# A hand-ordered two-layer kernel on one core: the skip term D of the first unit as rank-one matmuls, all spectral steps of two units summed, and a new instruction list

## The chip, the cores and the metric

The kernel runs on one core of a Trainium2 chip. Five engines work side by side, each through its own queue and strictly in the order in which its instructions were written: TensorE (PE in the profile; its weight loads are shown apart as PEld), VectorE (DVE), ScalarE (ACT), GpSimd (POOL) and SyncE (SP), which here does nothing but begin transfers. The metric is the device time of one execution in microseconds (us).

## The reference, cut to what matters

The input has 2048 positions of 640 channels, in bf16. Layer A normalises `q`, scales and shifts it by a modulation, and multiplies it by a long convolution; layer B is a gated MLP with a matmul over positions.

```python
k_shift = sum of 4 shifted copies of k, each times shift_k
kv = k_shift * v
y  = irfft(rfft(kv, 2S) * rfft(ssm_k, 2S))[:S]      # long convolution over positions, per channel
y  = y + kv * ssm_D                                 # skip term D, one number per channel
x  = x + ga * (LN(x)*(1+ca)+sa) * y                 # layer A
h  = LN(x)*(1+cb)+sb                                # layer B
z  = gelu(h @ w_in);  z1, z2 = halves;  z2 = LN(z2)
x  = x + gb * ((z1 * (w_sp @ z2 + b_sp)) @ w_out)
```

## The kernel before, in words

**Work and stages.** The 640 channels are cut into five *units* of 128 (`NU`, `DU`). For each unit, two sequences go through a Fourier transform made of matmuls: the filter (`XK`, from `ssm_k`) and the product `kv` (`XU`). A first stage (`stage1`, op `s1`) gives the tile `X1`; then come eight *steps* per sequence, each covering two blocks of frequencies:

- `fwd` on PE (`forward`): six matmuls into the PSUM tile `pu`. For the filter, ACT then copies the spectrum into the tile `KH` (`khc`).
- `prod` on DVE (line 454): the four real products of the spectrum of `kv` in PSUM with `KH`, 1024 elements in each partition.
- In a *summed* step (mode `s`) the products go to an f32 tile `Tf`, and two additions (`csum`, line 468, on POOL or DVE) turn them into the real and the imaginary part, tile `W`; the inverse (`inv`) is then six matmuls. In an *unsummed* step (mode `u`) the products go to a bf16 tile `T`, and `inv` does the additions itself, with twelve matmuls.
- `zc` copies the result of the inverse from PSUM to the tile `Z` on ACT or DVE.

After the eight steps `Z` is transposed (by a transfer `zt` for units 0 to 3, by PE in `last_stage_pe` for unit 4), and `y` (op `y` or `yl`) gives the convolution, which DVE multiplies into `gh` (`ym`, `yml`, lines 670 and 732). `gh` holds the modulated first normalisation (`xn`, `ghm`, line 653). The sum into `xt` is `res` (line 690), its statistics are `ln2`, `ag2`.

`kv` itself comes from transposing transfers of `k` and `v` (`load_kv`, op `ldk`), four tap matmuls (`taps`) with diagonal weights (`diag`), the product with `v` on DVE (`tv`, line 545), a write to DRAM (`kvw`) and a read in another layout (`load_X`, op `ldX`). The matrices of the transform are made on the chip: `F1` by DVE and ACT (`f1a`, `f1c`, `f1m`), `M2` by DVE, ACT and POOL (`turns`, `msub`, `msin`, `msgn`, `mneg`), `G2` by transposing `M2` (`gflip`, `gcopy`, `gneg`).

**The skip term** is put into the filter: `add_D` (op `addD`, line 392) adds D to position 0 of each channel's filter, after a chain in which D is loaded (`Dr`), spread (`dwide`), turned by PE (`turn1 tD`) and copied (`dcol`). Stage 1 of the filter waits for it.

**Layer B's first half** takes over after unit 4: normalisation (`zx`), a turn by PE (`hfl`) or by a transfer, modulation (`hmod`), the product with `w_in` (`zz`, 64 of five matmuls of 432 columns each, into `pu` or `pz`), `gelu` on ACT, normalisation `zn`. The second half (lines 961 to 1039) multiplies by `w_sp` (line 968) and `w_out` (line 989).

**What sets the order.** All of this up to the end of layer B's first half is registered as some thousand numbered operations with their dependences (class `Plan`). The string `ORDER` lists them, each with the engine that does it (P, A, D, G, S for PE, ACT, DVE, POOL, SP), and the kernel writes the instructions in just this order. So the list fixes each engine's queue and also which engine does an operation that several could do (the registered letters, `"GD"` for `csum`, say which may). PSUM tiles rotate: `pu`, `pz` and `sm` have two buffers each, `s1` one, so a matmul waits until the engine that reads the older tile is done. `FILLS` are matmuls without use, put into PE's queue at chosen places.

The choice of mode, and the inverse of a summed step:

```python
mode = MODE[u][st]; summed = mode == "s"
...
mm(p_[:, k], G2[:, 0, kc, :], w_[:, k], True, False)        # summed: 3 matmuls for each of 2 blocks
mm(p_[:, k, 1], G2[:, 2, kc, :], w_[:, k, 0], False, False)
mm(p_[:, k, 0], G2[:, 1, kc, :], w_[:, k, 1], False, True)
```

Of the kernel before, what the change touches and what calls it, by code (L numbers as in the profile page):

```python
# [11 lines left out]
BF16 = mybir.dt.bfloat16  # L12
# [3 lines left out]
P = 128  # L16
# [9 lines left out]
DU = 128  # L26
KP = 2
# [6 lines left out]
FILLS = (4, 3, 3, 2, 4, 3, )  # L34
MODE = ('susussus', 'susussus', 'susussus', 'susussus', 'susussus')
# [5 lines left out]
D0 G5 D13 S82 A1 S2 D15 D100 A4 D14 P1029 P7 G101 A16 D102 D109 D110 D6 D103 S19 D17 P1030 P8 D11 A111 A112 D121 D86  # L41
P1031 P145 A146 P148 A150 A149 D10 D23 D122 A123 D18 S88 G113 D90 S21 A124 G125 D147 D104 A106 G114 D115 S83 D87 A105
G126 P1032 P227 S20 A228 S22 P26 D27 P24 P154 A155 D116 A118 A117 S523 P151 A153 S34 D25 S32 P30 D31 P233 A234 P28 D29
S33 D152 A156 S35 G107 P133 D134 S84 S85 G119 G120 P139 P229 A140 S524 P161 D527 P163 A162 D528 G108 P136 D137 A164
P165 A166 P142 G48 A143 S46 S47 P157 A158 P169 A170 A230 G36 P37 P167 A168 G135 D529 P41 D530 P159 A160 D127 D38 G138
D144 P171 A172 P231 D42 D232 P173 P176 A175 A174 A177 P43 A178 D44 P182 A183 A184 P179 D181 P39 D40 S45 A180 P185 A531
D186 S3 P195 A532 A533 G187 P55 D196 P191 D192 D56 P211 P51 P247 A248 G197 G188 G198 P189 A190 P199 A200 P9 A12 D212
G213 D52 P205 D206 P201 P53 D202 G214 A534 D54 P49 D50 P217 S526 A542 A543 P245 A246 S89 D535 P193 A194 A544 G130 G131
S565 P251 G141 D218 D252 G72 P203 P221 D222 P239 A240 G207 G536 D537 P215 A204 G223 G224 A216 P253 D254 P568 P566 S525
P241 A242 P257 P225 A258 G553 G554 A569 P237 P249 G549 G550 A238 A250 S91 P255 A256 D538 D539 P219 S57 D226 D93 G208  # L50
D540 D541 P235 A236 P243 A244 P301 A302 A551 G60 G555 P259 P209 D260 G261 G262 A567 P291 D292 S570 G552 P303 S58 P269
A304 A220 D270 G271 S92 D210 P571 G272 D572 P285 D286 P307 A308 A545 P263 S59 P265 D266 P573 P63 P275 D276 A264 P305
A306 P293 A294 D546 P273 A274 D574 D649 P325 D64 G556 G287 D288 D709 D591 D651 G593 G547 D548 D557 D558 G559 G560 A326
P309 A310 P267 A268 P321 A322 P327 P315 A316 P65 D66 P319 A328 A561 G562 P61 D62 A320 A128 P295 S575 S70 D296 G297 S71
P329 A330 P576 P578 S94 D129 G298 D577 D592 D594 P313 A314 G653 P331 A332 D579 S599 P67 D68 P311 A312 A563 S69 S95
P289 A290 P333 D96 G564 D595 G596 P349 D711 P375 A376 P299 A300 D334 G335 G336 D350 P73 D74 S97 P379 A380 P77 P323
A324 P343 D344 P377 A378 P369 P337 A338 P351 A352 P317 A318 G597 G598 D78 G345 G346 P600 P381 D370 G371 P279 P347 G652
D601 P602 D280 G281 G282 A382 P277 D612 A348 P365 D603 D366 P79 D80 G655 P387 A278 P604 G372 A388 P399 A400 P359 P283
A284 P383 A384 D614 D605 P606 D360 D613 P401 P373 A402 G618 D619 P385 A386 D650 P353 P403 D354 A404 P339 G361 G362
D340 P75 D76 A374 P397 A398 P405 A406 G615 P367 D607 P395 A396 P407 D99 G616 D617 P449 S580 A450 A368 P413 G608 D408  # L60
P341 A342 P389 A390 P363 A364 D414 S620 P621 D672 P453 A454 G609 P393 A394 D622 P623 D624 P439 D440 G355 G356 S81 S98
P451 G409 P391 P625 P357 P427 A452 D626 P627 A392 D358 S657 G654 G410 P455 A456 P417 D428 P581 A582 D418 P411 A412
G676 G677 P457 A458 P473 A474 P471 A472 G429 D430 P443 P431 A432 P479 A480 P433 D628 P415 A416 G419 D444 S583 G629
D631 P475 A476 G420 P421 D434 P461 A462 P423 D670 D656 P477 A478 D424 P467 A468 G713 P658 D659 A422 P441 P463 A464
G445 D446 G671 P660 D661 G435 G436 A442 P481 D482 G634 D637 G674 P437 A438 P465 A466 P447 A448 P662 P497 P425 A426
P517 D663 P664 D498 G483 G484 P485 G675 D518 G519 A486 S754 P507 D508 D665 D633 P469 A470 P499 D509 A500 P459 A460
G520 G510 P501 D502 P521 G666 P487 D488 A522 S678 P511 A512 P513 D514 P584 A585 P491 G673 P489 A490 P515 G503 G504
A516 G712 P505 D492 G493 D494 D638 P679 D680 D635 G707 A506 P495 P681 D682 A496 P721 D630 G708 P683 D684 P719 D720
P685 A722 D686 G687 P717 P715 D716 A718 D632 S586 P587 A588 D688 D689 P723 D724 G710 D725 D727 D726 D756 D755 G757
D728 D729 D636 D730 D758 A759 P589 A590 P732 D733 G760 D690 D768 P746 G692 P1033 P1034 P761 D691 P762 D763 G667 D764  # L70
D765 A767 D731 D769 G770 P739 D734 D736 D738 A766 D695 D735 P813 A814 D771 G772 A773 D737 D833 D693 D696 D694 D832
S753 P781 P815 A816 P809 D831 A782 D834 G714 D747 P774 D777 D776 P775 A780 P788 G835 D836 G837 D840 A810 A789 A779
G838 D778 D740 D741 D744 D743 P791 A792 A839 S841 D697 G668 D701 D698 D700 P811 A812 P819 A820 P817 P795 D699 D745
# [970 lines left out]
```

## Time and profile before

| what | us |
|---|---|
| median of 3 runs (320.10 to 321.21) | 320.46 |
| the profiled execution, its own time | 320.46 |
| its span, from the first to the last instruction | 318.6 |
| around the span | 1.86 |
| PE busy | 307.7 |
| DVE busy | 209.3 |
| ACT busy | 146.2 |
| POOL busy | 124.1 |
| first product of unit 0 (`prod`) begins | 28.80 |
| last product of unit 4 ends | 119.16 |
| first matmul of layer B (`zz`) begins | 131.55 |
| first matmul of line 968 begins | 190.67 |

A line of a group gives the source line, the engine, the operation, the tiles (written <- read), the shapes (written <- read), the count after an x, the busy time, the mean duration in ns, and the idle time of that engine just before such instructions with what ended it. A line of the timeline begins with the start and the duration, both in us. A line of a table of windows gives the window, its length, the busy time of PE, PEld, DVE, ACT and POOL with the number of instructions, the granted clock, the share of the DMA engines and GB/s. The duration of a matmul includes its way through the array; so the time that a matmul costs PE is read from the distance between starts. On DVE and ACT, too, an instruction starts some 0.08 to 0.12 us before the one ahead of it has ended, when nothing is waited for.

### The profile page before, as it was taken

What the parts mean: (1) busy time and instruction counts of PE and PEld (TensorE: products, weight loads), DVE (VectorE), ACT (ScalarE), POOL (GpSimd) and SP (SyncE); (2) the same over time, 40 slices, a digit from 0 to 9 for tenths busy, and PEclk for the clock granted to TensorE, in tenths of its full rate; (3) what the DMA queues carried; (4) which work ended last, traced back from release to release, by engine and by line L of the source; (5) the groups of instructions that cost most, each with busy time, mean ns of one, the idle gap of its engine ahead of it and who ended that gap; (6) DMA issues with size and microseconds to landing.
All of it is one profiled execution on the core that took longest, in us unless ns stands there. A gap on an engine that the chain in (4) does not pass through costs nothing.

```text
span 318.6 us, 6407 instructions
## 1 busy us (share of the span) xinstructions
PE 307.7 (97%) x2575; PEld 203.5 (64%) x2575; DVE 209.3 (66%) x436; ACT 146.2 (46%) x259; POOL 124.1 (39%) x157
## 2 busy tenths in 40 slices
PE   7898999999999998999999999999999999999995
PEld 2475787878899987655555555555555555555554
DVE  8897999898999999997669682522222333323323
ACT  4889898987798755777657671000000000000001
POOL 2651879779988996884163310000000000000000
PEclk9999999999999999999999999999999999999999
DMA  8999999997967685030409980676557555522221
GB/s 162 223 224 256 273 289 191 224 250 175 229 173 141 238 161 217 2 71 14 83 0 159 192 202 19 132 156 117 116 115 117 115 117 115 115 51 49 49 51 62
DMA packets 127024, 44.99 MB, mean 141 GB/s; under 512 B 116143, under 2 KB 126228, under 8 KB 126996
## 3 DMA queue, kind: packets, MB, share of 16 engines
q1 hardware_dynamic: 126842, 44.55, 65.0%
q8 instruction: 20, 0.33, 0.4%
q14 instruction: 8, 0.07, 0.1%
q10 hardware_dynamic: 154, 0.05, 0.1%
HBM read 16.11 MB, written 5.24 MB: 67 GB/s over the span
## 4 chain that ended last, share of the span: by engine, by line
PE 75%; DVE 11%; SPq 6%; DMA 4%; POOL 2%; ACT 1%; issue 1%; DVEq 0%; POOLq 0%
PE ps L968 29%; PE pu L237 14%; PE pz L237 13%; PE po L989 9%; SPq L513 5%; PE sm L237 4%; DVE Tf L454 3%; PE s L237 3%; DMA big<-in_A_k_dram 2%; DVE T L454 2%; DMA X<-in_A_ssm_k_dram 1%; DVE big L545 1%; DVE X L240 1%; POOL W L468 1%; DVE T L337 1%
## 5 line engine op out<-in xcount | busy, mean ns | idle before, releaser
L968 PE MATMUL ps<-X,wT 128*128 128x432 bf16 x512 | 95.7, 346 | 0.0
L968 PEld LDWEIGHTS <-wT 128*128 128x128 bf16 x512 | 50.1, 98 | 42.2
L981 ACT COPY uT<-pt 128x896 bf16<-128x896 bf16 x1 | 0.9, 906 | 119.2 <-PE pt L980 119.2
L237 PEld LDWEIGHTS <-Z 128*128 128x128 bf16 x320 | 31.1, 98 | 26.8 <-DVE Z L857 0.2
L237 PE MATMUL pu<-X,M 128*128 128x128 bf16 (+1 forms) x480 | 45.9, 237 | 1.0 <-DVE Tf L454 0.5
L237 PEld LDWEIGHTS <-M 128*128 128x128 bf16 x480 | 37.6, 98 | 7.9 <-issue 2.2
L971 DVE SCALAR_TENSOR_TENSOR u<-ps,bcol,G 128x432 bf16<-128x432 f32 x18 | 12.0, 668 | 42.2 <-PE ps L968 42.2
L468 POOL TENSOR_TENSOR W<-Tf 128x256 bf16<-128x256 f32 x45 | 33.1, 752 | 16.0 <-DVE Tf L454 14.1
L237 PE MATMUL pu<-big,Z 128*128 128x432 bf16 x160 | 33.3, 346 | 0.0
L989 PE MATMUL po<-w_o,uT 128*128 128x320 bf16 (+2 forms) x231 | 33.2, 295 | 0.1
L237 PE MATMUL pz<-big,Z 128*128 128x432 bf16 x160 | 33.1, 346 | 0.0
L454 DVE TENSOR_TENSOR Tf<-pu,KH 128x1024 f32<-128x1024 f32 x25 | 30.3, 1219 | 2.1 <-PE pu L237 1.6
L240 ACT CAST X<-s 128x1024 bf16<-128x1024 f32 x29 | 29.7, 1024 | 3.7 <-PE s L237 3.4
L989 PEld LDWEIGHTS <-uT 128*128 128x128 bf16 (+1 forms) x231 | 22.2, 98 | 9.9 <-issue 0.2
L971 DVE SCALAR_TENSOR_TENSOR u<-ps,bcol,M 128x432 bf16<-128x432 f32 x14 | 9.3, 667 | 28.9 <-PE ps L968 28.9
L240 ACT CAST KH<-pu 128x512 bf16<-128x512 f32 x40 | 23.4, 598 | 6.2 <-PE pu L237 4.9
L237 PEld LDWEIGHTS <-G 128*128 128x128 bf16 x330 | 24.7, 98 | 1.8 <-issue 0.2
L991 DVE TENSOR_TENSOR ot<-po,xt 128x320 bf16<-128x320 f32 (+1 forms) x33 | 15.9, 481 | 12.6 <-PE po L989 12.6
L240 ACT CAST Z<-pz 128x512 bf16<-128x512 f32 x37 | 21.5, 596 | 5.6 <-PE pz L237 5.6
L237 PEld LDWEIGHTS <-X 128*128 128x128 bf16 x288 | 17.7, 97 | 6.7 <-DVE X L392 3.6
L237 PE MATMUL sm<-big,dg 128*128 128x512 bf16 (+1 forms) x80 | 20.2, 379 | 0.8 <-DMA big<-in_A_k_dram 0.8
L912 DVE BATCH_NORM_STATS2 stz<-X 128x6 f32<-128x432 bf16 x32 | 17.6, 585 | 4.4 <-ACT X L906 4.4
(150 smaller groups left out, 432.7 us busy)
## 6 DMA issues: line engine op xcount, KB each, us to landing
wm<-in_w_mod_dram SPq DMA_DIRECT2D x6, 800.0 KB, 6.9
xt<-in_A_q_dram SPq DMA_DIRECT2D x4, 640.0 KB, 5.8
out_dram<-ot SPq DMA_DIRECT2D x15, 160.0 KB, 2.3
big<-in_B_w_in_dram SPq DMA_DIRECT2D x2, 1080.0 KB, 7.8
X<-in_A_ssm_k_dram SPq DMA_DIRECT2D x4, 512.0 KB, 5.5
kv_scr<-big SPq DMA_DIRECT2D x4, 512.0 KB, 5.6
X<-kv_scr SPq DMA_DIRECT2D x4, 512.0 KB, 5.0
w_o<-in_B_w_out_dram SPq DMA_DIRECT2D x6, 160.0 KB, 3.2
```

Of the source, the lines that this page charges most:

```text
L237: nc.tensor.matmul(o, lhsT=w, rhs=x, start=start, stop=stop)
L240: (e.copy if e is nc.scalar else e.tensor_copy)(dst, src)
L337: op("D", "msub", lambda e: e.scalar_tensor_tensor(tl[a][:], tl[a][:], MAGIC, tl["mbase"][:, None].to_broadcast([P, 2, KCH, QH]), op0=ALU. ...
L454: e.tensor_tensor(T_[:], (tl[pu] if src is None else tl[src])[:, :, :, None, :].to_broadcast(shape), tl[KH][:, :, None, :, :].to_broadcast ...
L468: e.tensor_tensor(tl[W][:, :, o, :], T_[:, :, 0, o, :], T_[:, :, 1, 1 - o, :], op=ALU.add if o else ALU.subtract)
L513: e.dma_start_transpose(tl[name][:, o + h * m:o + (h + 1) * m], src[0, h * m:(h + 1) * m, dt * P:(dt + 1) * P])
L545: e.tensor_tensor(vsl, tl[ps][:], vsl, op=ALU.mult)
L912: op("D", "stz", lambda e, i=i, n=n, fc=fc: e.bn_stats(out=stz[:, n, fc, :], in_=tl[z2][:, i, fc * FC:(fc + 1) * FC]), r=[(z2, (i, fc))], ...
L968: nc.tensor.matmul(ps[:, :FC], lhsT=wTs[t][:, s_, :], rhs=tl["z2_%d" % (s_ // TB)][:, s_ % TB, fc * FC:(fc + 1) * FC], start=(s_ == 0), st ...
L971: nc.vector.scalar_tensor_tensor(u[:, sl], ps[:, :FC], bcol[:, t:t + 1], z1[t][:, sl], op0=ALU.add, op1=ALU.mult)
L989: nc.tensor.matmul(ps[:, :hi - lo], lhsT=uTs[t][:fsz[ft], ft, :], rhs=w_o[:fsz[ft], ft, lo:hi], start=(ft == 0), stop=(ft == NFT - 1))
L991: nc.vector.tensor_tensor(ot[:, lo:hi], ps[:, :hi - lo], xt[:, t, lo:hi], op=ALU.add)
```

## The change

1. **D of unit 0.** `add_D` is no longer called for unit 0. A tile `oneD` of one partition holds 128 ones (written by POOL) and D of the unit's 128 channels (one more small transfer, `ld1`, begun by SP). Each of unit 0's eight `fwd` of the filter gets one more matmul for each of its two blocks, with one row of weights, the ones, and the 128 values of D as the moving operand: it adds D to the real part of every frequency.
2. **Modes.** In units 0 and 1 all eight steps are summed, in place of five of eight; the other units stay as they are.
3. **First normalisation.** Tiles 2 and 3 (of each 8) may now be done by ACT as well.
4. **Fills.** Eight groups of 21 matmuls in place of six groups of 19: six groups with 16 before unit 0's spectrum is begun (before: four with 12), and two with 5 ahead of the first `yl` (before: two with 7 behind the third `yl`).
5. **A new list.** It assigns and orders everything anew. By engine it differs mainly in this: DVE gets 11 `csum` in place of 5, 19 `ghm` for 17, 4 `zc` for 3, 10 `zx` for 5, two `s1` copies more, 9 `zn` for 12 and one `xn`, one `gcopy`, the one `gneg`, the one `diag` and two `addD` fewer. POOL gets 51 `csum` for 45, 21 `ghm` for 23, 10 `xn` for 11, 2 `zx` for 7. ACT gets one `diag`, one `gcopy`, two `xn`, three `zn` more. On SP the order changes in few places: the new transfer of `oneD` stands after the second half of unit 0's filter, ahead of the second halves of `k` and `v` of unit 0; the small transfer of `c` moves from behind unit 1's `kvw` to ahead of unit 1's `v`; the load of `w_mod`'s first part moves ahead of `XU1`; the two halves of `w_in` change places.

```diff
-FILLS = (4, 3, 3, 2, 4, 3, )
-MODE = ('susussus', 'susussus', 'susussus', 'susussus', 'susussus')
+FILLS = (4, 3, 1, 2, 4, 2, 4, 1, )
+MODE = ('ssssssss', 'ssssssss', 'susussus', 'susussus', 'susussus')
...
+        oneD = consta.tile([1, 2, DU], BF16, name="oneD")
...
         def forward(name, X1, st, extra=()):
+            with_D = X1 == "X1K0"
+
...
-                    mm(pu[:, k, 1], M2[:, 1, kc, :], x[:, 2 * kc, :], False, True)
+                    mm(pu[:, k, 1], M2[:, 1, kc, :], x[:, 2 * kc, :], False, not with_D)
+                    if with_D:
+                        mm(pu[:, k, 0], oneD[:, 0], oneD[:, 1], False, True)
...
-            op("D" if n % 8 < 4 else "DA" if n % 8 == 4 else "A", "ln1", stats, r=xs, w=[("mv1", n), ("gh", (0, n // TB))], new=[(tile_, "st1")])
+            op("D" if n % 8 < 2 else "DA" if n % 8 < 6 else "A", "ln1", stats, r=xs, w=[("mv1", n), ("gh", (0, n // TB))], new=[(tile_, "st1")])
...
+        op("G", "dzero", lambda e: e.memset(oneD[:, 0], 1.0), w=[("oneD", 0)])
+        op("S", "ld1", lambda e: e.dma_start(oneD[:, 1], A_ssm_D[None, 0:DU]), w=[("oneD", 1)])
...
-            add_D(u)
+            if u:
+                add_D(u)
```

The queues of the new list where the prediction steps through them (numbers behind a name are unit and step; `s1 K0.0` is stage 1 of unit 0's filter, first quarter):

- PE, start: fill 4, `tsk`, fill 3, `s1 K0.0`, `s1 K0.4`, `taps 0.1`, fill 1, `tD`, fill 2, `s1 K1.0`, fill 4, fill 2, `s1 K0.12`, `s1 K0.8`, `s1 K1.4`, `taps 0.3`, `0.2`, `0.0`, then seven `fwd` of K0 among the four `gflip`, `s1 K1.12`, `tc`, `taps 1.3`, `s1 U0.0`, `U0.4`, `taps 1.0`, `s1 U0.8`, `U0.12`, `taps 1.2`, `fwd U0.0`.
- DVE, start: `ident`, `bits0`, `f1a`, `f1g`, `mstep`, `mbase`, `f1m`, `turns 1`, `turns 3`, `msub 3`, `dwide`, `msub 1`, `bits2`, `e2a`, `dcol`, `addD K1`, `turns 0`, `tv 0.1`, `msub 0`, `turns 2`, `msub 2`, `tv 0.3`, `mneg`, `tv 0.2`, `tv 0.0`.
- ACT, start: `silut`, `f1c`, `skc`, `diag 0`, all eight `s1` copies of K0 among the eight `msin`, one `s1` copy of K1, then the seven `khc` among three `gcopy`.
- End of unit 4: the last product is that of step 6 (unsummed; before, step 2, summed), then `inv 4.6`, `y`, `inv 4.2`, and the four turns `zfl` in the order 16, 24, 0, 8, of whose copies ACT does three and DVE one (before two each).

## The prediction, made before the changed kernel was run

> **What bounds the kernel now.** I read the page's first two parts first.
>
> ```profile
> span 318.6 us, 6407 instructions
> ...
> PE 307.7 (97%) x2575; PEld 203.5 (64%) x2575; DVE 209.3 (66%) x436; ACT 146.2 (46%) x259; POOL 124.1 (39%) x157
> ...
> PE   7898999999999998999999999999999999999995
> ...
> DVE  8897999898999999997669682522222333323323
> ```
>
> PE is busy nearly throughout, and behind 131.55 us (slice 17 on) its matmuls follow each other without a gap: the 64 `zz` and what follows cost what they cost, and neither their number nor their shape changes. So the change can act only by moving the moment at which `zz` begins. Before that moment DVE's row is as full as PE's. The table of windows, asked from the first product of unit 0 to the end of the last one of unit 4, says how full:
>
> ```profile
> 28.80:119.16 90.36, 88.13 (x1082) 74.99 (x1079) 85.11 (x123) 74.94 (x131) 77.22 (x88) 1.00 0.97 215
> ```
>
> Of 90.36 us DVE is busy for 85.11 and idle for 5.25. PE's 88.13 counts the way through the array. By distances between starts, its matmuls of this stretch leave some 6 us of gaps. POOL is idle for 13.1. So two engines with 94% each set the pace, and no wait among them is long: in the list of waits, PE's and DVE's longest here are 0.8 us.
>
> **The change part by part.** The prices:
>
> ```profile
> L468 POOL TENSOR_TENSOR W<-Tf 128x256 bf16<-128x256 f32 x45 | 33.1, 752 | 16.0 <-DVE Tf L454 14.1 <-DVE nmr L592 1.5 <-PE sm L237 0.3
> L454 DVE TENSOR_TENSOR Tf<-pu,KH 128x1024 f32<-128x1024 f32 x25 | 30.3, 1219 | 2.1 <-PE pu L237 1.6 <-ACT gh L568 0.2 <-issue 0.2
> ...
> L454 DVE TENSOR_TENSOR T<-pu,KH 128x1024 bf16<-128x1024 f32 x15 | 18.2, 1216 | 0.6 <-PE pu L237 0.4
> ...
> L653 DVE TENSOR_TENSOR gh<-gh,gca_bf 128x512 bf16<-128x512 bf16 x10 | 4.6, 488 | 0.1
> ...
> L468 DVE TENSOR_TENSOR W<-Tf 128x256 bf16<-128x256 f32 x5 | 2.2, 444 | 0.0
> ```
>
> These are groups by shape. The next lines are from the timeline at the end of unit 4:
>
> ```profile
> 117.39 1.93 PE L237 MATMUL pz<-T,G 128*128 128x256 bf16 x24
> ...
> 117.94 1.22 DVE L454 TENSOR_TENSOR Tf<-pu,KH 128x1024 f32<-128x1024 f32 x1
> ...
> 119.15 0.60 PE L237 MATMUL pz<-W,G 128*128 128x256 bf16 x6
> 119.19 0.42 DVE L468 TENSOR_TENSOR W<-Tf 128x256 bf16<-128x256 f32 x1
> 119.24 0.96 POOL L468 TENSOR_TENSOR W<-Tf 128x256 bf16<-128x256 f32 x1 [0.18 <-DVE Tf L454]
> ...
> 119.53 0.42 DVE L696 BATCH_NORM_STATS2 st<-xt 128x6 f32<-128x256 bf16 x1
> 119.59 0.40 PE L237 MATMUL sm<-Ebd,ZT 128*128 128x64 bf16 x8
> ```
>
> *PE.* Two unsummed inverses begin at 117.39 and end where the next begins, 119.15: 0.88 each. The summed one lasts to 119.59: 0.44. Six steps change: 6 x 0.44 = 2.65 less. The product costs the same in either form (1.219 and 1.216). The 16 matmuls for D are in no row. A matmul of 128 columns takes (0.442 - 2 x 0.11)/4 = 0.056 from start to start (four of 256 columns take 0.45), and four of 5 columns take 0.13. So 16 cost from 0.5 to 1.8 (as if of 256); I take 0.056, the same columns, so 0.9; never a gain, as PE's queue grows. Two fills of 0.215 (half of 0.86 for a tap group of four, twice) add 0.4, mostly into waits. Sum on PE: -1.3.
>
> The Trainium skill, "TensorE: Matmul & The Clock Gate", section "Back-to-back issue gap", gives about 81 ns for a matmul of 128 columns in a stream with weight loads, where this trace has 56. By it D would cost 1.3 in place of 0.9; the trace decides.
>
> *DVE, the load that decides.* I counted both lists from the first product to the last, those included: 111 operations before, 122 after. Prices are durations less the 0.08 to 0.1 by which neighbours overlap (the last `csum` above runs 0.34 to the next start):
>
> - `csum` 4 -> 11: 7 x 0.34 = +2.35
> - `ghm` 17 -> 19: 2 x 0.42 = +0.84
> - `tv` 12 -> 13: +0.60; `zc` 3 -> 4: +0.58; `res` 0 -> 1: +0.34
> - `xn` 2 -> 1: -0.36
>
> Sum +4.36. Products, `ym`, `s1` copies, `ln1` are equal in number. So DVE has 85.11 + 4.36 = 89.5 us to do where 90.36 were used. The two D additions of unit 0 (0.39 each) go, but lie ahead of this stretch.
>
> *POOL* has six `csum` more (4.3), but one `ghm`, one `xn`, one `res`, a `gneg` and the preparation of `sc` fewer: -0.9 in the same stretch, under 13.1 of idle time. It waits for DVE's products (14.1 of its 16.0), not the other way round.
>
> One row shows what two sums at a time cost: at 119.19 DVE's takes 0.42, POOL's beside it 0.96, against a median of 0.73 for POOL. So POOL pays, by 0.23. The Trainium skill, "SBUF — State Buffer", section "SBUF: two separate sides", speaks against this change harder: DVE and GpSimd have one port pair in common, and a DVE operation with two SBUF inputs and a GpSimd one that reads SBUF block each other for a whole instruction. By that, each of seven more DVE sums could wait for one on POOL, 7 x 0.73 = 5.1 more; DVE's five (415 to 526 ns) show no such wait.
>
> *The head, up to the first product.* Today stage 1 of K0 waits for the D addition until 6.92. In the new queue it needs only `F1` and the filter, which landed at 4.21. `F1` comes after six DVE operations: about 4.3; so stage 1 starts at 4.75, behind the fill, 2.2 earlier. What then hides that gain is ACT: `diag` (four multiplications of 128 columns, in no row: from 0.18 each, as 5 columns cost, to 0.41, as 256 do; I take 0.25, the sum 1.0), all eight K0 copies (0.48 each) and eight `msin` (0.41) stand in its queue. By their sums the first spectrum copy begins at about 15.6. Then seven `khc` (0.485) and three `gcopy` (0.91) hold PE to ACT's pace until about 22.5. XU0 decides: its read is issued at 20.42 behind transfers that fill SP without a break. `oneD` (issue 0.56) and `c` (0.38) now stand ahead of it: later by 0 (if the long issues of the transposing transfers are a full queue, as the DMA share of 1.0 suggests) to 1.0. The taps that feed it end about 0.8 earlier, which could make it earlier by at most that. I take +0.5 for the transfer, +0.2 for the first product (29.0): before, 4.2 us lie between stage 1 of U0 and `fwd U0.0`; the new queue has one tap group fewer there.
>
> *The end of unit 4.* The last product is now of an unsummed step: its inverse waits for no sums, but takes 0.88. I get the first turn 2.4 behind the last product (before 121.53 - 119.16 = 2.4). From there to `zz` the old chain has 3.6 to the first `yl`, 5.0 to `hfl`, 1.4 to `zz`. The new one has three ACT copies of 1.0 in place of two, +0.25, and 0.4 fewer fills: 0, bounds -0.5 and +0.5.
>
> **The sum.** `zz` moves by 0.2 (start) + 4.36 (work) - 5.25 (the old idle time) + the new idle time of DVE = -0.7 + idle. PE's own work in this stretch falls by about 1 (one `s1`, one tap group and one `fwd` of K0 move in, 2.65 goes), so PE stops pressing and DVE waits less than before. But the queues stay locked to each other through two `pu` buffers, and today's best 10-us windows of DVE have 9.8 busy. At 97%, 89.5 us need 92.2: idle 2.7. So **+2.0**: the profiled execution took 320.46, equal to the median; **322.5**.
>
> **Rivals.**
>
> - *The idle time of DVE closes almost wholly (about 0.7).* For it: PE has slack, so DVE has a queue of ready work. Against: 99% is above every window of today. 320.46 + 0 = 320.5, no change.
> - *Faster: the head's gain arrives.* Stage 1 of K0 starts 2.2 earlier; if the taps' 0.8 carries over to XU0 and the first product begins at 28.0, and idle is 0.3, `zz` moves by -0.8 - 0.9 + 0.3 = -1.4: 319.0. It decides if XU0's issue begins before 20.2. Against: the DMA engines are full from 10 to 70 us, and two issues more stand ahead.
> - *The waits stay (5.25).* Nothing of the old idle time is used, since each wait belongs to a place in the order: -0.7 + 5.25 = +4.6, 325.0. Against: PE has less to do.
> - *The change doesn't do what it says:* PE's 2.65 less arrives nowhere, since DVE sets the pace. That is part of the forecast already; only with PE alone as the bound would it be -1.3 (319.2), which the 94% of DVE excludes without the head's gain.
>
> **How the numbers follow.** A measurement of this kernel tells 0.3% (1 us) from no change. Forecast, idle from 1.7 to 4 (321.5 to 323.8): 0.43. Waits stay, 324 and above: 0.15. Closed, within 1 us: 0.20. Faster: 0.22. So faster 0.22, same 0.20, slower 0.58. The forecast alone spans 321.5 to 323.8; the range goes to 319.0, leaving out half of the faster case, and to 325.4, the waits kept plus the end's 0.5.
>
> **What would show it.** DVE busy about 89.5 us between first and last product and at least 97%, while PE's gaps there grow beyond today's 6 us, ended by DVE's products; the first product near 29.0; the last one ending near 121.2; `zz` beginning near 133.6 and no gap behind it. Wrong I am if the first product comes before 28.3, if DVE's busy time there is below 87, or if gaps appear among the `zz`.

## The result, and the profile after

The changed kernel takes 325.62 us (median of 4 runs, 325.15 to 326.59), the kernel before 320.83 beside it (4 runs, 320.10 to 321.63): a ratio of 1.0153, 95% interval 1.0116 to 1.0189, so some 4.9 us slower. The forecast was 322.5 with a range to 325.4: the direction was right, the size was not, and the time lies just above the range. The profiled execution took 325.84, its span is 324.0 (before 318.6).

The page's first parts, in the kernel after:

```profile
span 324.0 us, 6396 instructions
...
PE 311.7 (96%) x2557; PEld 204.2 (63%) x2557; DVE 208.7 (64%) x440; ACT 152.2 (47%) x269; POOL 122.7 (38%) x157
...
PE   7899998999999989899999999999999999999995
...
DVE  7687999999989999878657673433322222233333
...
PEclk9999999999999999799999999999999999999999
```

PE is busy for 4 us more although it has 18 matmuls fewer (16 for D and 2 fills more, 36 of the six inverses fewer): either matmuls became dearer or the clock fell. The row PEclk shows one place of the second kind, the 17th slice (129.6 to 137.7 us), where the granted clock is 0.7 of full speed; before it is full there. DVE's row is thinner in the first three slices and fuller after: the work begins later, then it is denser.

The window from the first product to the end of the last one, in the kernel after, with the columns as before:

```profile
31.86:122.62 90.76, 87.26 (x1054) 73.44 (x1052) 88.95 (x135) 75.98 (x132) 75.94 (x88) 1.00 0.91 204
```

DVE is busy for 88.95 of 90.76 us; 5.25 us of idle time have become 1.81. The groups of that window by shape:

```profile
L460 DVE TENSOR_TENSOR Tf<-pu,KH 128x1024 f32<-128x1024 f32 x31 | 37.4, 1218 | 1.2 <-ACT KH L241 0.7 <-PE pu L238 0.3
...
L474 DVE TENSOR_TENSOR W<-Tf 128x256 bf16<-128x256 f32 x11 | 4.8, 447 | 0.1
```

Six products have moved to the summed form at the same price (1218 ns), and eleven sums on DVE take 447 ns on average, as five took 444 before. One of the eleven, with two operations of POOL beside it, takes 772 ns; the other ten take 409 to 425.

Where the 5.4 us of span came from, by the moments that the prediction used (from the start of the span; distances from unrounded times):

| | before | after | predicted | difference measured |
|---|---|---|---|---|
| first product begins | 28.80 | 31.86 | 29.0 | +3.06 |
| first to last product | 90.36 | 90.75 | 92.2 | +0.39 |
| last product to `zz` | 12.39 | 13.08 | 12.4 | +0.69 |
| `zz` to the end | 187.02 | 188.34 | 187.0 | +1.32 |

**The head.** The timeline in the kernel after, PE and its weight loads in the first transform of K0:

```profile
17.45 0.09 PEld L238 LDWEIGHTS <-oneD 1*128 1x128 bf16 x1
17.45 0.22 PE L238 MATMUL pu<-oneD 1*128 1x128 bf16 x1
17.60 0.22 PEld L238 LDWEIGHTS <-M 128*128 128x128 bf16 x3
17.61 0.39 PE L238 MATMUL pu<-X,M 128*128 128x256 bf16 x3
17.93 0.09 PEld L238 LDWEIGHTS <-oneD 1*128 1x128 bf16 x1
```

Read the weight loads. Between equal matmuls a load begins some 0.05 ahead of its matmul, beside the matmul in front. The load of `oneD` begins only with its own matmul, and the load behind it, too. From one matmul for D to the next it takes 17.45 to 17.93, 0.476 unrounded, for half a transform; its other three matmuls alone take 0.222. So one matmul for D costs 0.254, and sixteen cost 4.1 us, in a queue of PE that is unbroken from 17.06 to 26.33. Over the same stretch ScalarE waits for PE five times (0.36 to 0.78).

**Ahead of it** PE stands still once more than I had counted. The timeline of PE, kernel after:

```profile
9.22 0.60 PE L238 MATMUL s<-F1bd,X 128*128 128x256 bf16 x4
11.19 1.67 PE L238 MATMUL s<-ident 128*128 128x512 bf16 x6 [1.37 <-ACT X L241]
```

The six matmuls at 11.19 are fillers: the fifth and sixth group of `FILLS`, of 4 and 2, which the experiments call fillers 4 and 5, counting from 0. They write the PSUM tag `s1`, which has one buffer, so a filler waits for ScalarE's copy of the stage 1 at 9.22; taps, `kvw` and `XU0` come behind it.

### The profile page after: what moved, and what is told of

Its sections match the earlier page's. It is cut to its first block, busy times and chain, and to the rows that moved or that the text cites. A ratio compares the mean times of both kernels' runs of the same rounds, so it can differ in the third digit from the quotient of the medians.

```text
span 324.0 us, 6396 instructions
## 1 busy us (share of the span) xinstructions
PE 311.7 (96%) x2557; PEld 204.2 (63%) x2557; DVE 208.7 (64%) x440; ACT 152.2 (47%) x269; POOL 122.7 (38%) x157
## 4 chain that ended last, share of the span: by engine, by line
PE 77%; DVE 13%; ACT 4%; issue 2%; DMA 2%; POOL 0%; DVEq 0%; POOLq 0%; ACTq 0%
PE ps L977 29%; PE pu L238 17%; PE pz L238 12%; PE po L998 9%; PE s L238 5%; DVE Tf L460 4%; PE sm L238 4%; DMA Z<-Z 2%; ACT X L241 2%; DVE big L551 2%; DVE gh L676 1%; DVE T L460 1%; DVE gh L659 1%; DVE st L702 1%; DVE X L241 1%
## 5 line engine op out<-in xcount | busy, mean ns | idle before, releaser
L238 PE MATMUL pu<-X,M 128*128 128x128 bf16 (+1 forms) x480 | 47.1, 237 | 2.6 <-DVE Tf L460 1.9
L474 POOL TENSOR_TENSOR W<-Tf 128x256 bf16<-128x256 f32 x51 | 37.0, 749 | 9.5 <-DVE Tf L460 6.0
L460 DVE TENSOR_TENSOR Tf<-pu,KH 128x1024 f32<-128x1024 f32 x31 | 37.4, 1218 | 1.2 <-ACT KH L241 0.7
L238 PE MATMUL pz<-big,Z 128*128 128x432 bf16 x160 | 32.3, 346 | 0.2 <-ACT X L915 0.2
L241 ACT CAST X<-s 128x1024 bf16<-128x1024 f32 x28 | 28.6, 1021 | 3.9 <-PE s L238 3.8
L238 PEld LDWEIGHTS <-G 128*128 128x128 bf16 x294 | 22.3, 98 | 3.0 <-issue 0.8
L241 ACT CAST Z<-pz 128x512 bf16<-128x512 f32 x36 | 20.6, 596 | 5.8 <-PE pz L238 5.7
L238 PEld LDWEIGHTS <-X 128*128 128x128 bf16 x288 | 18.8, 99 | 5.9 <-issue 2.2
L238 PE MATMUL sm<-big,dg 128*128 128x512 bf16 (+1 forms) x80 | 20.9, 388 | 0.0
L659 POOL TENSOR_TENSOR gh<-gh,gsa_bf 128x512 bf16<-128x512 bf16 x15 | 17.9, 1198 | 6.8 <-DVE gh L659 6.3
```

Source lines behind the costliest of these rows:

```text
L238: nc.tensor.matmul(o, lhsT=w, rhs=x, start=start, stop=stop)
L241: (e.copy if e is nc.scalar else e.tensor_copy)(dst, src)
L460: e.tensor_tensor(T_[:], (tl[pu] if src is None else tl[src])[:, :, :, None, :].to_broadcast(shape), tl[KH][:, :, None, :, :].to_broadcast ...
L474: e.tensor_tensor(tl[W][:, :, o, :], T_[:, :, 0, o, :], T_[:, :, 1, 1 - o, :], op=ALU.add if o else ALU.subtract)
L659: lambda e, vec=vec, o=o: e.tensor_tensor(gvu, gvu, vec[:, None, d0:d0 + du].to_broadcast([P, TB, du]), op=o),
```

## The experiments

Times from the traces; "stretch" is first product to end of the last, "idle" DVE's idle time in it. The ratio is to the kernel before, timed beside it on the same chip.

The trace figures are of one execution each, and two pairs of rows say how far such figures scatter. "128 rows, gelu first" has the same instructions as "D in 128 rows" up to the end of the stretch, yet its stretch is 2.45 longer. "Before, DVE loaded" has the same head as "before", yet its first product comes 1.06 later (its `XU0` is issued at 21.69, not at 20.42). A part of the scatter can be seen. At first PE runs at half its pace (in the kernel after, the stage 1 matmuls at 4.94 start 0.21 apart, those at 12.70 0.11). Where the trace has the clock rise at 7.1 us or later, the first transform of the new list (fillers 4 and 5 kept) begins at 17.05 to 17.07; where it rises at 5.5 or earlier, at 16.24 to 16.51.

| kernel | ratio, 95% interval | first product | stretch | idle | `zz` to end |
|---|---|---|---|---|---|
| before | 1 | 28.80 | 90.36 | 5.25 | 187.0 |
| after | 1.0153, 1.0116 to 1.0189 | 31.86 | 90.75 | 1.8 | 188.3 |
| D in 128 rows | 1.0100, 1.0060 to 1.0140 | 29.58 | 90.69 | 1.9 | 188.7 |
| D by row count | one run, 323.78 us | 30.52 | 90.74 | 1.8 | 188.0 |
| D left out | 1.0104, 1.0050 to 1.0159 | 28.74 | 92.27 | 3.2 | 188.0 |
| two fillers out | 1.0112, 1.0062 to 1.0162 | 29.27 | 90.72 | 1.8 | 188.4 |
| both cures | 1.0071, 1.0044 to 1.0099 | 30.27 | 92.41 | 2.8 | 188.5 |
| three cures | 1.0095, 1.0060 to 1.0130 | 29.36 | 95.17 | 5.9 | 189.2 |
| old modes | 1.0149, 1.0111 to 1.0188 | 31.87 | 92.81 | 5.6 | 187.7 |
| end fillers back | 1.0117, 1.0072 to 1.0163 | 31.09 | 91.42 | 2.9 | 188.4 |
| after, DVE loaded | 1.0187, 1.0160 to 1.0214 | 31.86 | 93.14 | 1.2 | 188.9 |
| gelu first | 1.0132, 1.0098 to 1.0165 | 31.87 | 90.74 | 1.8 | 188.2 |
| 128 rows, gelu first | 1.0113, 1.0073 to 1.0152 | 29.03 | 93.14 | 3.5 | 188.5 |
| before, one-row matmuls | 1.0036, 1.0016 to 1.0056 | 33.35 | 88.81 | 4.3 | 187.0 |
| before, DVE loaded | 1.0131, 1.0104 to 1.0158 | 29.86 | 94.49 | 4.2 | 187.2 |
| before, sums | 1.0275, 1.0245 to 1.0305 | 29.23 | 98.89 | 10.2 | 186.7 |

### What the matmuls for D cost, and why

**D in 128 rows.** The tile gets 127 rows of zeros, for both operands.

```diff
-        oneD = consta.tile([1, 2, DU], BF16, name="oneD")
+        oneD = consta.tile([128, 2, DU], BF16, name="oneD")
...
-        op("G", "dzero", lambda e: e.memset(oneD[:, 0], 1.0), w=[("oneD", 0)])
+        def ones(e):
+            e.memset(oneD[:], 0.0)
+            e.memset(oneD[0:1, 0], 1.0)
+        op("G", "dzero", ones, w=[("oneD", 0)])
...
```

> The changed kernel, with the tile of D padded with zeros from 1 row to 128, so that the 16 matmuls of D contract over 128 rows like their neighbours; nothing else differs and the sum is the same. Theory A (a matmul of one row among matmuls of 128 rows costs about 0.25 us, because its weight load and its stream do not overlap with the neighbours): a forward transform of K0 falls from 0.87 to about 0.55 us, PE's queue of the head ends some 3 us earlier, the first product comes at 29.5 to 30.5 instead of 31.86, and the time falls by 1.5 to 2.5 us. Rival B (any matmul of 128 columns put behind the four of 512 columns costs that, whatever its rows): the transform stays at 0.87 and the time within 0.5 us of the changed kernel. Rival C (XU0's transfer decides the first product): the transform gets shorter, but the first product stays at 31 to 32.

The same place in its timeline:

```profile
17.30 0.10 PEld L238 LDWEIGHTS <-oneD 128*128 128x128 bf16 x1
17.36 0.22 PE L238 MATMUL pu<-oneD 128*128 128x128 bf16 x1
17.36 0.26 PEld L238 LDWEIGHTS <-M 128*128 128x128 bf16 x3
17.41 0.38 PE L238 MATMUL pu<-X,M 128*128 128x256 bf16 x3
...
17.63 0.22 PE L238 MATMUL pu<-oneD 128*128 128x128 bf16 x1
```

The load now begins 0.06 ahead of its matmul, and from this matmul to the next it takes 0.055: from one matmul for D to the next it is 17.36 to 17.63, 0.278 unrounded, so D costs 0.056, what the prediction took. Theory A holds; B is out, and so is C, which had the first product at 31 or later. The first product comes 2.28 earlier; the first transform begins at 17.06 in both. The ratio falls from 1.0153 to 1.0100, 1.7 us. With the padded rows the transfer of `XU0` does set the moment: in both profiles with this one cure in the head the first product follows its issue by 8.01 to 8.02 (21.57 and 29.58; 21.02 and 29.03).

**D by row count.** The same tile; `oneD[0:n]` with n = 1, 32, 64, 96 for steps 0 and 1, 2 and 3, 4 and 5, 6 and 7.

> The changed kernel, with the tile of D padded with zeros to 128 rows, and the D matmuls of the eight steps of K0 contracting over 1, 1, 32, 32, 64, 64, 96, 96 rows. It prices a row count. Theory A (only a weight of all 128 rows overlaps): all steps cost about 0.87 us. Rival (the price is that of one row alone, or falls with the rows): 0.87 for the first two, and from some row count on 0.55. The 96-row matmuls elsewhere in this kernel show no price (14 of 320 columns in 1.91 us), so I expect 96 rows to be cheap and the break between 1 and 64.

The timeline of PE with 64 rows, and with 96:

```profile
23.77 0.23 PE L238 MATMUL pu<-oneD 64*128 64x128 bf16 x1
...
24.26 0.23 PE L238 MATMUL pu<-oneD 64*128 64x128 bf16 x1
...
24.65 0.22 PE L238 MATMUL pu<-oneD 96*128 96x128 bf16 x1
...
24.93 0.22 PE L238 MATMUL pu<-oneD 96*128 96x128 bf16 x1
```

From one matmul for D to the next it takes 0.49 with 64 rows and 0.28 with 96; with 1 and 32 rows it is 0.48 too. So the price is not that of a row or of a count: it is paid in full up to 64 rows and not at all at 96. Theory A, that only all 128 rows overlap, is too strict. Why the break lies there is not shown.

The Trainium skill, "TensorE: Matmul & The Clock Gate", section "The mechanism", says that a weight load runs beside a matmul in flight only when their row groups (the strips of 32 rows that they use) differ; the same section also lets a load be pulled ahead when the groups don't conflict or when it goes to a background buffer for weights. Here loads of 128 rows behind matmuls of 128 rows overlap (0.056 from start to start), which the first sentence by itself excludes; loads of 1, 32 and 64 rows among them don't (0.25), and neither sentence tells 64 rows from 96. The measurement decides.

**D left out.** `with_D = False`; the D term of unit 0 is missing in the output.

> The changed kernel without the 16 matmuls of D in unit 0: the D term of the first unit is left out of the output. Theory A (they hold PE for about 4 us of the head, and the first product behind them): a forward transform of K0 takes 0.44 us, the first product comes 1.5 to 2.5 us earlier than 31.86, the time falls by as much. Rival C (XU0's transfer, landed at 25.03, decides): stage 1 of U0 begins at 27.2 as before, or at most 0.3 earlier, and the time is within 0.5 us.

The transform takes 0.44, and the first product comes 3.1 earlier, at 28.74, more than expected; 0.8 of it is that the first transform begins at 16.24 here and not at 17.06, ahead of any matmul for D. The rest agrees with the 2.28 of the padded rows, and so does the time. Rival C is out: stage 1 of `U0` begins at 24.13, not at 27.2. Stretch and idle time are 1.5 longer, with DVE waiting 0.60 for the transfer of `xt` at 44.8. That the transfers ask back later what the engines gained in front is a reading and not shown, as two profiles of the same stretch differ by more.

**The kernel before with one-row matmuls.** Sixteen matmuls of one row of zeros behind the transforms of K0.

```diff
...
-                    mm(pu[:, k, 1], M2[:, 1, kc, :], x[:, 2 * kc, :], False, True)
+                    mm(pu[:, k, 1], M2[:, 1, kc, :], x[:, 2 * kc, :], False, X1 != "X1K0")
+                    if X1 == "X1K0":
+                        mm(pu[:, k, 0], oneD[:, 0], oneD[:, 1], False, True)
```

> The kernel before, with 16 matmuls of one row of zeros (one weight row, 128 columns) behind the transforms of K0, as the changed kernel has them; they add zeros, D stays on DVE. Nothing else differs. Theory A (the one-row matmul is what costs 0.25 us, in any list): a K0 transform takes 0.87 instead of 0.44 and PE's queue of the head gets 4 us longer; as PE has idle time in this head, part of it is hidden: the first product comes 1 to 3 us later than 28.8, and the time is 1 to 3 us above the kernel before. Rival B (the list, not the matmul, makes the head late): the time is within 0.5 us of before.

Two matmuls for the zeros in its first transform:

```profile
17.95 0.23 PE L237 MATMUL pu<-oneD 1*128 1x128 bf16 x1
...
18.43 0.22 PE L237 MATMUL pu<-oneD 1*128 1x128 bf16 x1
```

The price goes with the matmul, not with the list: a half transform takes 0.48, and the first product comes 4.55 later (4.0 for the matmuls, 0.5 by which this run was already late at the first transform, 17.63 in place of 17.09; in it the clock rose only at 11.31, in the kernel before at 6.50). That is more than the 1 to 3 expected. The time rises by 0.36% only, 1.2 us, at the lower end of what was expected. Of the 4.55, 1.55 come back in its trace between first and last product. The other difference is that the one profile of the kernel before took 320.46, while the median beside this run is 322.24.

### What else delays the head

**Two fillers out.** Fillers 4 and 5 are left out (`FILLS = (4, 3, 1, 2, 4, 1, )`, the last two being those at the end).

> The changed kernel without its fillers 4 and 5, which stand early in PE's queue in front of the first transforms (6 filler matmuls; they add nothing to the result). Theory D (the first of them waits 1.5 us for ScalarE's copy, since the fillers share one PSUM buffer with stage 1; that delays taps, kvw and so XU0): XU0's transfer is issued about 1.5 us earlier (19.9 instead of 21.4), and the first product and the time come 1 to 1.8 us earlier. Rival E (PE's D matmuls absorb it: ScalarE's copies set the pace of the transforms anyway): time within 0.5 us.

Without them `s1 K0.12` begins at 9.95 in place of 12.70, `kvw` is issued at 15.72 and 16.31 in place of 16.66 and 17.60, `XU0` at 20.72 in place of 21.39. The first product comes 2.59 earlier, the time falls by some 1.3 us. Theory D holds for PE's queue and the first product; the effect on `XU0` (0.67, not 1.5) is within its scatter, as the nine profiles with these fillers have it between 21.01 and 21.83. In SP's queue the issue of the transposing transfer in front of it takes 3.32 here and 2.91 in the kernel after.

**Both cures.** D in 128 rows and two fillers out.

> The changed kernel with both cures of the head: the tile of D padded with zeros to 128 rows, and fillers 4 and 5 left out. Alone the first brought the first product from 31.86 to 29.58, the second to 29.27. If PE's queue of the head is all there is, they add: 27.5 or less. If XU0's transfer decides next (theory C): 28.2 to 28.8. In both cases the stretch of the products stays at 90.7, as DVE is busy in all but 1.8 of it, and the time is 0.5 to 1.5 us below that with one cure, still 1 to 2.5 us above the kernel before: what is left is DVE's load and the way from the last product to zz.

They don't add. The first product comes at 30.27, later than with either. The timeline of PE:

```profile
21.07 0.17 PE L238 MATMUL sm<-ident,KH 5*128 5x5 bf16 x1 [1.56 <-DMA KH<-in_c_dram]
```

This is the turn of `c`, which the new list puts in the middle of K0's transforms; that PE comes to it earlier does not make its transfer land earlier. And behind the pause the granted clock of the window 22 to 26 is 0.58, so the next matmuls cost more. Of all variants of the changed list this has the lowest ratio, 1.0071, but its interval overlaps those of the single cures (1.0100 and 1.0112), so that it is better than one cure is not shown.

**Three cures.** The same, with `c`, its turn and what hangs on it moved behind the first inverses of unit 0 (in `ORDER`; no code changes).

> The changed kernel with D padded to 128 rows, fillers 4 and 5 left out, and a third cure: the transfer of c, its turn on PE and what hangs on it (silu, two copies on POOL) moved behind the first inverses of unit 0, about where the kernel before has them. With two cures PE waited 1.56 us for the transfer of c in the middle of the K0 transforms, and the first product came at 30.27. Theory C (the wait for c is what stopped the two cures from adding): no wait of PE for c, the transforms of K0 end by 21.5, XU0's issue comes some 0.4 earlier, the first product at 27.7 to 28.7, 2 us earlier than with two cures, and the time 1 to 2 us below theirs (ratio to before 1.000 to 1.004). Rival J (XU0 waits for the slots of the transfer queue, with or without c): first product at 29 or later, and the time within 0.5 us of two cures.

PE no longer waits for `c`, and the transforms end at 23.0, but the first product comes only at 29.36: `XU0` is issued at 21.49 as in the kernel after (21.39), and PE waits 0.74 for it. That is rival J by the first product; the ratio can't be told from that of two cures (1.0095 and 1.0071). `XU0`'s issue lies between 20.72 and 21.83 in all variants of the new list, whatever PE does. In the stretch DVE now waits 1.44 for the transfer of `xt` and 0.84 for a filter; the stretch is 95.17. The profiled execution (328.22) is the longest of its six (median 324.76): PE also waits 1.52 in it for unit 0's filter, and the clock falls to 0.50 at 11.49. So I take the places of the waits from it and not their size.

### Products and sums

**Old modes.** The changed kernel with `MODE` of the first two units as before: 12 `csum` go, 9 of them on POOL.

> The changed kernel with the modes of the first two units as before: their steps 1, 3 and 6 are not summed; 12 csum go (3 on DVE, 9 on POOL), and these six inverses have 12 matmuls instead of 6 (+2.65 us on PE). Theory H (DVE's load sets the pace of the products): from first product to last it takes 0.5 to 1.0 us less than 90.75, DVE's busy time falls by 1.0. Rival I (PE has become the bound as well): 0.5 to 1.5 us more. The head's 31.86 stays in both.

The window from first product to last:

```profile
31.87:124.68 92.81, 89.27 (x1084) 75.96 (x1088) 87.23 (x132) 76.17 (x132) 69.11 (x79) 1.00 0.90 199
```

DVE has 1.7 less to do and the stretch is 2.06 longer: idle time 5.58 in place of 1.81. Rival I holds, beyond its 1.5, and H falls. PE's 2.65 of longer inverses come back as DVE's waiting: DVE waits 2.7 for the spectrum in `pu`, in the kernel after 0.7, and no transfer is among its waits. In the time the two kernels can't be told apart (1.0149 and 1.0153).

**DVE loaded.** Twelve statistics operations on DVE in either kernel, with a result that nobody uses.

```diff
+                if u and st in (2, 5, 7):
+                    e.bn_stats(out=pnum[:], in_=M2[:, 0, 0:2, :].rearrange("p k f -> p (k f)"))
```

> The kernel before with 12 more statistics operations on DVE (128x256 columns of a constant, 0.42 us each by the row of ln2, 0.36 by the distance of starts), one behind the product of steps 2, 5 and 7 of units 1 to 4; their result is used by nobody. So DVE gets the 4.3 us that the change gives it, and PE keeps its load. Theory K (DVE and PE are locked: idle time of DVE is what PE's load leaves it): DVE's idle time of 5.25 between first and last product closes only in part, the stretch grows by 2 to 4 us from 90.36 and the time by as much. Theory H (DVE has room until it is full, as the changed kernel's stretch of +0.39 suggests): idle falls to about 1.8, the stretch grows by 0.5 to 1.

> The changed kernel with the same 12 statistics operations more on DVE, 4.3 us. If DVE is the bound there (idle 1.8 of 90.75 between first product and last): the stretch grows by 3.8 to 4.5 us and the time by 3.5 to 4.5, to a ratio of 1.026 to 1.030 to the kernel before. If the order of the queues or PE sets the pace: by less than 2.5.

Their windows from first product to last, the kernel before first, and then the changed one:

```profile
29.86:124.34 94.48, 88.47 (x1074) 74.93 (x1078) 90.25 (x135) 74.98 (x131) 77.38 (x88) 1.00 0.93 206
```

```profile
31.86:125.01 93.15, 87.85 (x1048) 73.63 (x1052) 91.90 (x147) 76.06 (x132) 75.82 (x88) 1.00 0.89 201
```

In the kernel before, 5.1 us more DVE work lengthen the stretch by 4.1 (idle time 5.25 to 4.23) and the time by 1.3%, 4.2 us: theory K, a little beyond its 4, not H. DVE has no room there even though it idles. In the changed kernel 2.95 us more in the window lengthen it by 2.4, which is just under the 2.5 that was to tell DVE alone as the bound from the order or PE. Its time is 1.0187 of before; against 1.0153 that is less than the 3.5 expected, with intervals that overlap.

So it takes both loads to see the +0.39. In the kernel before, DVE work passed into the stretch at 0.8 (4.1 of 5.1); at that rate the 3.84 us that the change adds are worth 3.1. In "old modes" PE's 2.65 lengthened the stretch by 2.06 though DVE had 1.7 less, worth 1.4; so PE's are worth some 3.4. The two cancel, as an estimate from single profiles, to -0.3.

**The sums alone, in the kernel before.** `MODE` of the changed kernel; nine of the 12 sums on POOL, three on DVE, right behind their products; the inverses in the order of the products.

> The kernel before with one part of the change alone: all steps of the first two units summed (six more; their 12 csum 9 on POOL and 3 on DVE, as in the changed kernel, in the queues behind their products; the inverses of these units follow in the order of the products; one negation on POOL comes a few places earlier). D, the head and the end stay as before. PE has 2.65 us less, DVE 1.0 more, POOL 6.6 more. In the changed kernel the same sums shortened the products' stretch by 2.06 us against the old modes. Theory K (PE and DVE are locked, and PE's load is the dearer): the stretch from first product to last falls by 1 to 2 us from 90.36, and the time falls below the kernel before by as much. Rival L (DVE's load sets the pace): it grows by up to 1.0. Rival M (POOL's sums come too late for the inverses with two W buffers, as PE waits for them): it grows by 1 us or more, and PE's waits for POOL's W show it.

2.75% slower. The longest wait of DVE in the stretch of that kernel (engine, tile and line, what it waited for, us in total, times, longest):

```profile
DVE nmr L593 <- POOL rstd L186: 3.8, 2, 3.6
```

POOL's `rstd` of the first normalisation stands behind sums that wait for products (1.71 and 1.44 us just ahead of it), and DVE waits for it. That is 3.8 of the 8.5 by which the stretch grows; DVE also waits 3.5 for PE, and the clock falls to 0.50 for 3.41 us at 44.90. Rival M holds in kind, but mainly through POOL's queue and not through the inverses, for which PE waits 0.9. It says that the sums need a list made for them; it doesn't price them.

### The end

**End fillers back.** Fillers 6 and 7 behind the third `yl` again.

> The changed kernel, with its fillers 6 and 7 (5 filler matmuls, 1.3 us) moved on PE from in front of the first yl to behind the third yl, in front of hfl, where the kernel before has its last two. Theory F (the fillers stood where no wait was, and left PE idle for 1.2 us in front of hfl, after which the granted clock fell to 0.55 and the first zz were slow): no gap in front of hfl, granted clock 1.00 from 132 to 140, the first yl at most 0.5 earlier because ScalarE's copies then end its wait, zz the same or up to 0.5 earlier; time 0.3 to 1.2 us below the changed kernel. Rival G (the chain through LayerNorm sets zz, fillers or not): zz and the time within 0.3.

F falls, and it is worse than G expected. There is no gap in front of `hfl` now, but PE waits 0.34 and 0.56 for ScalarE's copies ahead of `yl`, the clock falls all the same, to 0.50 from 132 to 134, and `zz` begins 14.04 behind the last product, not 13.08. The fillers stand in this fall themselves (the five take 2.26 to their end, in the kernel after 1.46), so which place is better for the way to `zz` is not shown; the time itself can't be told from that of the changed kernel. (Fillers 6 and 7 are the last two groups, of 4 and 1.)

**The fall of the clock.** Two windows at the end of unit 4, in the kernel after and in "two fillers out", cut at the same distance from the first `zz`; PE's busy time stands behind the length, the granted clock third from the end:

```profile
132.00:134.00 2.00, 0.95 (x34) 0.86 (x33) 1.93 (x9) 1.03 (x2) 0.69 (x1) 1.00 0.00 0
134.00:138.00 4.00, 4.00 (x50) 2.78 (x51) 3.13 (x11) 2.42 (x5) 1.97 (x4) 0.57 0.02 4
```

```profile
129.00:131.00 2.00, 1.27 (x36) 1.06 (x34) 1.89 (x8) 0.66 (x1) 0.98 (x2) 1.00 0.00 0
131.00:135.00 4.00, 3.68 (x54) 2.54 (x55) 3.45 (x13) 2.74 (x6) 1.92 (x4) 1.00 0.00 0
```

Ahead of `hfl` PE waits 1.05 for ScalarE's `zx` in both. In one the clock then falls to 0.57 for 4 us and the first ten matmuls of `zz` take 2.75 us; in the other it stays and they take 1.98 (before: 1.82). The clock fell near there in 8 of the 12 profiles of the new list and in none of the 4 of the old list, which has no such wait. Eleven of the 12 have the wait of 1.05, and 7 of these the fall, within 2 us behind the wait; the twelfth, "end fillers back", has the fall without the wait. So the wait neither suffices nor is needed; what decides stays open.

The means of the windows hide how the clock falls. In each of the 11 falls that lie whole inside a profile it goes to 0.50 and stays there for 3.41 us (in the kernel after from 134.20), and in all 16 profiles its changes lie whole multiples of 3.41 us apart (126.29 is 37 of them, 317.44 is 93). The first change comes between 4.67 and 11.31 us, so the points at which the clock changes lie differently against the same instructions from execution to execution. That alone does not settle it either: PE is busy for 2.36 of the 3.41 us up to 134.20 in the kernel after, where the fall follows, and for as much up to 132.21 in "two fillers out", where none does.

The Trainium skill, "TensorE: Matmul & The Clock Gate", section "HAM oscillation — how this bites in real kernels", states as the rule that PE must not be idle for more than about 3.4 us. Here no wait of PE near the fall was longer than 1.05, and in the kernel after PE was busy for 0.95 of the 2 us ahead of `hfl`.

**Gelu first.** Where the clock stayed, PE waited instead. The timeline of PE in "two fillers out":

```profile
136.65 1.07 PE L238 MATMUL pu<-big,Z 128*128 128x432 bf16 x5 [0.69 <-ACT M L915]
```

ScalarE does a second `zx` (0.92) ahead of gelu's table load (1.28) and the first gelu; before, that `zx` stands behind the first gelu. Moved back:

> The changed kernel with one operation moved on ScalarE: the second normalisation zx of the second group (0.92 us) goes behind the first gelu instead of ahead of it, as in the kernel before. Theory N (the new list lets gelu's table load of 1.28 us and the first gelu begin 0.9 later, and PE's third zz in pu waits 0.69 for it): the wait of 0.69 goes, and from zz to the end it takes 187.2 to 187.7 instead of 188.0 (188.3 and more where the clock falls); time 0.5 to 0.9 below the changed kernel. Rival O (hfl of the second group then waits for the moved zx): the wait only changes its place, time the same.

> Both cures whose gain was seen or is expected alone: D padded with zeros to 128 rows (alone ratio 1.010 to the kernel before), and the zx of gelu_first moved. Theory N: first product at 29.5, no wait of 0.69, time 0.5 to 0.9 below that of the padded rows alone, ratio 1.007 to 1.009. What is left is then DVE's load and XU0's transfer.

The clock fell in both profiles, and then gelu waits for PE with or without the move: `zz` to the end 188.2 and 188.5. Neither time can be told from that of its partner (1.0132 and 1.0153; 1.0113 and 1.0100). So theory N is neither shown nor refuted. What is shown is that the first 40 matmuls of `zz` take 8.81 in the kernel after (with the fall), 8.87 in "two fillers out" (with the wait) and 7.86 before: about 1.0 is lost either way. In the five profiles whose fall begins within 0.6 us of the first `zz`, they take 9.5 to 9.7. In the times the fall can't be seen: the kernel after took 325.15 and 325.84 with a mean clock of 0.993 and 0.995, 325.40 and 326.59 with 1.000. A small wait near 165 adds 0.37.

No variant beats the kernel before.

## Why the prediction was wrong

- **What bounds the kernel: right.** The moment of `zz` decides for most of it: of 5.4 us, 4.1 have arisen by then.
- **The head, "+0.2 (29.0)": wrong, and this is the step that failed.** The term is "16 matmuls for D, I take 0.056, bounds 0.5 to 1.8". They cost 0.254 each, 4.1. I priced by columns and never by rows of weights. The lower bound came from four matmuls of five rows that follow one another, where each starts 0.03 to 0.06 behind the last (the first line below). The trace of before had a better row: the one turn of `c`, five rows among 128-row neighbours.

```profile
3.47 0.29 PE L237 MATMUL sm<-ident,KH 5*128 5x5 bf16 x4
...
34.25 0.09 PEld L237 LDWEIGHTS <-KH 5*128 5x128 bf16 x1
34.25 0.17 PE L237 MATMUL sm<-ident,KH 5*128 5x5 bf16 x1
...
34.36 1.06 PE L237 MATMUL pu<-X,M 128*128 128x256 bf16 x12
```

  The load of this one begins with its own matmul, not ahead of it. The matmul starts 0.152 behind a matmul whose likes give way after 0.055, and the next one follows 0.106 later, with only five columns. So it cost 0.152 + 0.106 - 0.055 = 0.20, and 16 of them 3.2 or more, outside my bounds. With the price I took (the padded rows) the first product comes at 29.58. There it follows the issue of `XU0`, 21.57 against the 20.92 that I took, and that is the other 0.6; what share of it is the list's and what scatter is not shown.
- **The path through ScalarE, and the fillers "+0.4, mostly into waits": wrong.** Stage 1 did start early, at 4.94 (forecast 4.75). But I had PE held to ScalarE's pace up to 22.5, with the first spectrum copy at 15.6. It began at 18.19, and ScalarE waited for PE. I had missed that the fillers wait for ScalarE through the one `s1` buffer: without two of them the copy begins at 15.37 and the first product comes 2.59 earlier. In "both cures" this and the 2.28 of D don't add; `c`'s transfer, the fall of the clock behind it and `XU0` stand in the way there.
- **`XU0` "+0.5 of 0 to 1.0": the upper end** between these two profiles, 20.42 to 21.39. The four profiles of the old list have its issue from 19.45 to 21.69, so the delay by the list itself is not shown.
- **DVE's load, "89.5, +4.36": right.** It is 88.95, +3.84. That DVE's sums show no wait beside POOL's was read from five; of the eleven one does (772 ns).
- **"New idle time 2.7": too much**, measured 1.81. The reason given was right: PE lets go as its work falls ("old modes": 2.06).
- **"End of unit 4: 0, -0.5 to +0.5": nearly.** It is +0.31 in nine variants, 0.69 here, where the clock fell earlier.
- **"Behind `zz` no gap": wrong by 1.3.** The prediction held matmuls of equal number and shape to cost the same. About 1 was lost to the clock, or, where it held, to a wait for gelu, whose start is later; 0.37 to a small wait.
- **The rivals.** "The waits stay" gave 325.0, near the measured time for another reason: the waits went, the head came late. Its size is no support for it. "Faster" would have needed `XU0` before 20.2; no variant of the new list reached that.

The sum with the measured terms: 3.06 + 0.39 + 0.69 + 1.32 = 5.46 on the span of 318.6, against +2.0 forecast. Of the miss of 3.46, 2.9 lie in the head, 1.3 behind `zz`, 0.7 at the end of unit 4, less 1.4 in the stretch. A microsecond at the first product is not one at the end: in the kernel before 4.5 of it cost 3.0 between the two profiles and 1.2 by the medians, and in the changed one 2.3 to 3.1 bring back 1.3 to 1.7. So the price of D is the term of the sum that missed by most (4.1 for 0.9), but its cure alone does not bring the time back: with the padded rows the ratio is still 1.0100.

## What to carry to other kernels

Price a small matmul by its rows of weights as well as its columns, and look in the trace for one of such a shape among its neighbours: when its weight load starts with its own matmul and not ahead of it, nothing hides the load, and a price taken from a run of equal small matmuls does not hold; padding to the neighbours' rows with zeros can be the cheaper form. An idle engine has room only if the one it waits for gives way: test both loads. When several queues are packed tightly, ask of each cure what comes next (here PE, then `c`, then `XU0`), and don't add up gains at a point in the middle as if they reached the end. One profile is one execution: before a difference of a microsecond is read, compare two profiles of the same instructions.

## What the runs showed of the hardware that was not expected

- Among 128-row matmuls of 128 columns, one more of 1, 32 or 64 rows costs 0.25 us, of 96 or 128 rows 0.056.
- The granted clock fell to 0.50 for 3.41 us within 2 us of a wait of only 1.05, in 7 of 11 profiles with the same instruction order around it, and once without that wait. All its changes in 16 profiles lie whole multiples of 3.41 us apart.
- Four matmuls of five rows behind one another start 0.03 to 0.06 apart; a single one among 128-row neighbours cost 0.20.
- One small transfer, placed where PE turns its data early, stopped PE for 1.56 us once the work ahead of it got shorter, and the clock fell to 0.58 behind that wait.
